# Three token tiles instead of two in step at the start of a linear-attention and gMLP mixer

## The chip, the core and the metric

The kernel runs on one core of a Trainium2 chip. The metric is the time of one execution in microseconds (us), measured on the device. TensorE (PE in the profile) multiplies matrices into PSUM; VectorE (DVE), ScalarE (ACT) and GpSimd (POOL) read PSUM or SBUF and do the element-wise work; SyncE (SP) here only issues DMAs, as ScalarE does for some.

## What is computed

Two mixers run on the same input x of 2048 tokens by 512, and a per-token gate mixes them. The reference, cut to what matters:

```python
def _A_ref(x, wqkv, w_phi, wo):          # B, S, D = 1, 2048, 512; 32 heads of 16
    q, k, v = split(x @ wqkv)
    pq, pk = q @ w_phi, k @ w_phi        # per head
    phi_q = concat([softmax(pq), softmax(-pq)])
    phi_k = concat([softmax(pk), softmax(-pk)])
    kv, z = phi_k.T @ v, phi_k.sum(tokens)
    return ((phi_q @ kv) / (phi_q @ z + 1e-06)) @ wo
def _B_ref(x, w_in, w_sp, b_sp, w_out):  # F = 1376, Fh = 688
    z = gelu(x @ w_in)
    z1 = z[..., :Fh]
    z2 = layernorm(z[..., Fh:])
    g = w_sp @ z2 + b_sp[:, None]        # over the 2048 tokens
    return (z1 * g) @ w_out
g = sigmoid((x * gate_w).sum(-1, keepdims=True))
return g * _A_ref(...) + (1 - g) * _B_ref(...)
```

## The kernel before

The tokens are cut into 16 tiles of 128. A first stage makes z2 and z1 of every tile: x @ w_in in its two halves of 688 columns, through GELU. A second stage runs attention and the product with w_sp over the stored tiles and writes the output. The order of the instructions on TensorE and ScalarE is the order in which the program writes them; on VectorE and the queues a scheduler decides, and it prefers copies marked high priority.

**The contraction.** x @ w_in contracts over 512, in four blocks `dt` of 128. The right half of w_in (688 columns, for z2) lies in SBUF as `w_z2[:, dt, :]`, and "block dt" below is its 128 by 688 piece. One token tile of z2 takes eight matmuls: four blocks by two column halves `j` of 344 (`z_one`, L190). The second half has one column more, 345, for the gate's logit; `gate_T` (L284) puts gate_w into that column by a tiny transpose on TensorE and a copy on VectorE (L287). z1 uses the left half, `w_z1`, in the same way.

**x transposed.** The matmuls need x with its features on the partitions (`xT`). For tokens of tiles 4 to 15 a DMA transpose brings it (L130 one tile each, L139 four tiles). For tiles 0 to 3 a plain load brings x into `xs`; `x_T` (L274) then transposes 128-column pieces on TensorE (L276) into a PSUM tile from the pool's two `pq` buffers, and VectorE (L282) or ScalarE (L279) copies the result into `xT`.

**PSUM for z.** There are three `zp` tiles of two banks, taken in turn. After a tile's eight matmuls, `z2_out` (L203) runs GELU on ScalarE (L205), the copy of the gate logit to `glog` on VectorE (L206), and the batch-norm statistics on VectorE (L208, L209). A zp tile is free for its next user after GELU and the glog copy. z1 tiles use the same three buffers and only GELU (L256).

**The opening.** `z2_first_two` (L214) writes the order by hand: filler matmuls on constants (`warm_up`, L221), the transposes of x tiles 0 and 1, then blocks 0 and 1 of the first column half of both tiles, the gate, block 2, the second column half, and x tile 2's transposes; then tile 0 and tile 1 are finished, and x tile 3 is transposed. The first pair of transposes of x tile 1 writes to an extra PSUM tile `tp1` that borrows the third zp. After it, `z2_tile(2)` and `z2_tile(3)` run alone, and then a loop over chunks of four tiles: z2 (from the second chunk on), z1, and the normalisation (L263 to L268).

**The queues.** Two DMA queues carry the first loads. On Sync's: x tile 0 (L119), x tile 1 (L121), x tiles 2 and 3 in one DMA (L123), the second half of block 0 (L126), the transpose for tile 4 (L130), the two halves of w_z1 (L134), then the further transposes. On ScalarE's: the first half of block 0 (L120) and blocks 1, 2, 3 (L117). These DMAs signal on eight completion semaphores in turn, so the ninth is issued once the first has landed. GpSimd's queue brings gate_w (L113).

**Later.** `load_out_weights` (L423) loads w_out and wo into parts of `wspT` that the second stage has finished with; wo comes as two DMAs (L430).

Of the kernel before, what the change touches and what calls it, by code (L numbers as in the profile page):

```python
# [11 lines left out]
BF16 = mybir.dt.bfloat16  # L12
I32 = mybir.dt.int32

P = 128
# [4 lines left out]
F = 1376  # L20
FH = 688
HF = FH // 2
NT = S // P
NDT = D // P
# [11 lines left out]
def kernel(  # L36
# [14 lines left out]
    nc = tc.nc  # L51
    x2 = A_x.flatten_outer_dims()
# [11 lines left out]
    w_z2 = early.tile([P, NDT, WP], BF16, name="w_z2")  # L64
# [26 lines left out]
    xs = early.tile([P, 4, D], BF16, name="xs")  # L91
# [4 lines left out]
    w_in_v = B_w_in.rearrange("(dt p) f -> p dt f", p=P)  # L96
# [7 lines left out]
        out=ramp[:, 0, :], data0=ones32[:, :], data1=zeros[:, :], initial=0.0,  # L104
# [4 lines left out]
    for q in range(4):  # L109
        qs = slice(32 * q, 32 * q + 32)  # L110
        nc.vector.tensor_tensor(
            out=ident[qs, qs], in0=ramp[qs, 0, :], in1=ramp[qs, 1, :], op=ALU.is_equal)
# [3 lines left out]
    def load_z2w(eng, dt):  # L116
        eng.dma_start(out=w_z2[:, dt, 0:FH], in_=w_in_v[:, dt, FH:F])  # L117

    nc.sync.dma_start(out=xs[:, 0, :], in_=x2[0:P, :])  # L119
    nc.scalar.dma_start(out=w_z2[:, 0, 0:HF], in_=w_in_v[:, 0, FH:FH + HF])  # L120
    nc.sync.dma_start(out=xs[:, 1, :], in_=x2[P:2 * P, :])  # L121
    load_z2w(nc.scalar, 1)
    nc.sync.dma_start(  # L123
        out=xs[:, 2:4, :], in_=x2[2 * P:4 * P, :].rearrange("(i p) d -> p i d", p=P))
    load_z2w(nc.scalar, 2)
    nc.sync.dma_start(out=w_z2[:, 0, HF:FH], in_=w_in_v[:, 0, FH + HF:F])  # L126
    load_z2w(nc.scalar, 3)

    def x_dma_T(i):
        nc.sync.dma_start_transpose(out=xT[:, :, i * P:(i + 1) * P], in_=x2[i * P:(i + 1) * P, :])  # L130

    x_dma_T(4)
    for h in range(2):
        nc.sync.dma_start(  # L134
            out=w_z1[:, 2 * h:2 * h + 2, :], in_=w_in_v[:, 2 * h:2 * h + 2, 0:FH])
    for i in range(5, 8):
        x_dma_T(i)
    for q in range(2, NCH):
        nc.sync.dma_start_transpose(  # L139
            out=xT[:, :, q * CH:(q + 1) * CH], in_=x2[q * CH:(q + 1) * CH, :]  # L140
        )
    nc.sync.dma_start(out=brow[0:NT, :], in_=B_b_sp.rearrange("(t p) -> t p", p=P))
    for qk in (1, 0):
        nc.sync.dma_start_transpose(
            out=wqkT[:, qk * NDT:(qk + 1) * NDT, :], in_=A_wqkv[:, qk * D:(qk + 1) * D])
# [4 lines left out]
    for h in range(2):  # L150
        nc.sync.dma_start(
            out=wv_sb[:, 2 * h:2 * h + 2, :],
            in_=A_wqkv[h * 2 * P:(h + 1) * 2 * P, 2 * D:3 * D].rearrange("(dt p) n -> p dt n", p=P),
        )
    for q in range(NCH):
        nc.sync.dma_start_transpose(
            out=wspT[:, :, q * CH:(q + 1) * CH], in_=B_w_sp[q * CH:(q + 1) * CH, :]
# [4 lines left out]
        out=mask4[:], in_=mask4[:], pattern=[[-32, NG]],  # L162
# [3 lines left out]
        out=mask4[:], in_=mask4[:], pattern=[[32, NG]],  # L166
# [3 lines left out]
        out=mask64[:, :, :], in_=mask4[:, :, None].to_broadcast([P, NG, DH]))  # L170
# [4 lines left out]
    psA = psA_cm.__enter__()  # L175
    turn = {"zp": 0, "pq": 0, "mm": 4}

    def next_turn(kind, n):
        turn[kind] += 1
        return f"{kind}{(turn[kind] - 1) % n}"  # L180

    def zp_tile():
        return psA.tile([P, 2, CH], FP32, name="zp", tag=next_turn("zp", 3))

    def pq_tile(shape, dtype=FP32):
        return psF.tile(shape, dtype, name="pq", tag=next_turn("pq", 2))

    def z_one(zp, tt, wt, w, dt, j, first=0):
        n = HF if j == 0 else w - HF
        nc.tensor.matmul(  # L190
            zp[:, j, 0:n], lhsT=xT[:, dt, tt * P:(tt + 1) * P],
            rhs=wt[:, dt, j * HF:j * HF + n],
            start=(dt == first), stop=(dt == NDT - 1),
        )

    def z_mm(tt, wt, w):
        zp = zp_tile()
        for dt in range(NDT):
            for j in range(2):
                z_one(zp, tt, wt, w, dt, j)  # L200
        return zp

    def z2_out(tt, zp):  # L203
        z2v = z2all[:, tt, :].rearrange("p (j n) -> p j n", j=2)
        nc.scalar.activation(out=z2v, in_=zp[:, :, 0:HF], func=AF.Gelu_apprx_tanh)  # L205
        nc.vector.tensor_copy(out=glog[:, tt:tt + 1], in_=zp[:, 1, HF:HF + 1])  # L206
        for j in range(2):
            nc.vector.bn_stats(out=bn6[:, tt, j, :], in_=z2v[:, j, :])  # L208
        nc.vector.bn_aggr(out=mv[:, tt, :], in_=bn6[:, tt, :, :].rearrange("p j s -> p (j s)"))  # L209

    def z2_tile(tt):
        z2_out(tt, z_mm(tt, w_z2, FH + 1))

    def z2_first_two():  # L214
        zps = [zp_tile() for _ in range(2)]
        tp1 = psA.tile([P, 2, P], BF16, name="tp1", tag=next_turn("zp", 3))
        turn["zp"] -= 1

        def warm_up(n, w=CH):
            for _ in range(n):  # L220
                nc.tensor.matmul(  # L221
                    zps[0][:, 1, 0:w], lhsT=nc.const_aps.tensor(1.0, [P, P], BF16),
                    rhs=nc.const_aps.tensor(1.0, [P, w], BF16), start=True, stop=True)

        def one(tt, dt, j):
            z_one(zps[tt], tt, w_z2, FH + 1, dt, j, first=j)

        warm_up(6)
        warm_up(2, P)
        x_T(0, 0, 1, pq_tile([P, 1, P], BF16)[:, :, :])  # L230
        x_T(0, 1, NDT, pq_tile([P, 3, P], BF16)[:, :, :])
        warm_up(3, P)
        one(0, 0, 0)
        x_T(1, 0, 2, tp1[:, :, :])
        x_T(1, 2, NDT, pq_tile([P, 2, P], BF16)[:, :, :], on_act=True)
        one(0, 1, 0)
        warm_up(1, P)
        one(1, 0, 0)
        one(1, 1, 0)
        gate_T()  # L240
        one(0, 2, 0)
        one(1, 2, 0)
        for dt in range(1, 3):
            one(0, dt, 1)
            one(1, dt, 1)
        x_T(2, 0, NDT, pq_tile([P, NDT, P], BF16)[:, :, :])
        for tt in range(2):
            one(tt, 3, 0)
            one(tt, 0, 1)
            one(tt, 3, 1)  # L250
            z2_out(tt, zps[tt])
        x_T(3, 0, NDT, pq_tile([P, NDT, P], BF16)[:, :, :])

    def z1_tile(tt):
        zp = z_mm(tt, w_z1, FH)
        nc.scalar.activation(  # L256
            out=z1all[:, tt, :].rearrange("p (j n) -> p j n", j=2), in_=zp[:, :, 0:HF],
            func=AF.Gelu_apprx_tanh,
        )
# [14 lines left out]
    def x_T(i, d0, d1, tp, on_act=False):  # L274
        for dt in range(d0, d1):
            nc.tensor.transpose(tp[:, dt - d0, :], xs[:, i, dt * P:(dt + 1) * P], ident[:, :])  # L276
        dst = xT[:, d0:d1, i * P:(i + 1) * P]
        if on_act:
            nc.scalar.copy(out=dst, in_=tp)  # L279
        else:  # L280
            with tc.high_priority():
                nc.vector.tensor_copy(out=dst, in_=tp)  # L282

    def gate_T():  # L284
        gt = pq_tile([P, NDT])
        nc.tensor.matmul(gt[:, :], lhsT=gaterow[:, :], rhs=ident[:, 0:NDT], start=True, stop=True)
        nc.vector.tensor_copy(out=w_z2[:, :, FH], in_=gt[:, :])  # L287

    def b_T():
        bt = pq_tile([P, NT])  # L290
        nc.tensor.matmul(bt[:, :], lhsT=brow[:, :], rhs=ident[:, 0:NT], start=True, stop=True)
        nc.vector.tensor_copy(out=bT[:, :], in_=bt[:, :])
# [20 lines left out]
        return [lambda: take(dst[:, 2], banks[2]), lambda: take(dst[:, 3], banks[3])]  # L313

    with tc.manual_schedule(engines={mybir.EngineType.PE, mybir.EngineType.Activation}):
        z2_first_two()
        z2_tile(2)
        z2_tile(3)
        for c in range(NCH):
            ts = list(range(c * 4, c * 4 + 4))  # L320
            for tt in ts:
                if c > 0:
                    z2_tile(tt)
                if c >= 2 and tt % 4 == 1:
                    later = fold(3 - c)
            for tt in ts:
                z1_tile(tt)
                if c >= 2 and tt % 2 == 0:
                    later.pop(0)()
            z2_norm(ts)  # L330
            if c == 1:
                b_T()
# [90 lines left out]
    def load_out_weights():  # L423
        slabs = wspT[:, :, 0:D]
        w_main = [slabs[:, 0:5, :], slabs[:, 5:10, :]]
        w_rem, wo_t = slabs[:, 10, :], slabs[:, 11:11 + NDT, :]
        nc.gpsimd.memset(w_rem, 0.0)
        for h in range(2):
            gs = slice(2 * h, 2 * h + 2)
            nc.sync.dma_start(  # L430
                out=wo_t[:, gs, :],
                in_=A_wo[h * 2 * P:(h + 1) * 2 * P, :].rearrange("(g p) n -> p g n", p=P))
        for i in range(2):
            nc.sync.dma_start(
                out=w_main[i],
                in_=B_w_out[i * REM:i * REM + 5 * P, :].rearrange("(ft p) n -> p ft n", p=P),
            )
        nc.sync.dma_start(out=w_rem[0:REM, :], in_=B_w_out[5 * P:FH, :])
        nc.sync.dma_start(out=w_rem[P - REM:P, :], in_=B_w_out[0:REM, :])
        return w_main, w_rem, wo_t  # L440
# [95 lines left out]
    with tc.manual_schedule(engines={mybir.EngineType.PE, mybir.EngineType.Activation}):  # L536
# [3 lines left out]
        for tt in range(NT):  # L540
# [7 lines left out]
            if tt == 7:  # L548
                w_main, w_rem, wo_t = load_out_weights()
# [51 lines left out]
```

The softmax here doesn't subtract the row's maximum and nothing guards it: scores larger than these inputs give would overflow.

## Time and profile before

| what | value |
|---|---|
| median of 5 runs | 208.56 us (208.14 to 209.03) |
| the profiled execution's own time | 208.72 us |
| its span, first to last instruction | 207.0 us |
| TensorE busy | 202.7 us, 98% |
| VectorE busy | 129.5 us, 63% |
| ScalarE busy | 76.5 us, 37% |
| GpSimd busy | 45.3 us, 22% |
| z stage's matmuls (L190), 256 of them | 39.3 us busy |

The span leaves out 1.72 us of the profiled execution's time, which lie around its first and last instruction. In the timelines a line gives start, duration, engine, source line, operation, what it writes and reads, shape and count; in square brackets stands how long the engine was idle before it, and what ended that. Matmuls overlap each other: the stated duration of one is its way through the array, and the distance from one start to the next is what it holds the engine for. DMA issues are listed with their size and the median time from issue to landing.

### The profile page before, as it was taken

The page shows a single profiled execution, that of the slowest core. Times are in us where ns is not written, and L with a number is a line of the kernel's source. Part 1 is how long each engine was busy: PE and PEld are TensorE (multiplying, and loading weights), DVE is VectorE, ACT ScalarE, POOL GpSimd, SP SyncE. Part 2 cuts the span into 40 slices and gives each one's busy share as a digit, 9 for nine tenths or more (in the row PEclk, how much of TensorE's full clock was granted, in tenths as well). Part 3 has the DMA queues.
Part 4 walks back from the last instruction along what each step waited for, and adds up shares of the span by engine and source line. Part 5 has one row for each costly group of instructions (what it writes and reads, how often), then busy time and mean ns, then how long its engine had stood idle before and what let it go on. Part 6 is the DMA issues. An engine that isn't in the chain of part 4 may idle for free.

```text
span 207.0 us, 3966 instructions
## 1 busy us (share of the span) xinstructions
PE 202.7 (98%) x1544; PEld 120.9 (58%) x1544; DVE 129.5 (63%) x278; ACT 76.5 (37%) x123; POOL 45.3 (22%) x73
## 2 busy tenths in 40 slices
PE   8999999999999999999999999999999999999994
PEld 4566666655566555556565666555455555665642
DVE  3377756655977778879797788555466553633330
ACT  2666678786422232333323033222251126001322
POOL 5020202020542326243342422222204220200000
PEclk9999999999999999999999999999999999999999
DMA  6999399999995024971413226753564667453642
GB/s 186 271 225 193 85 232 209 254 180 273 179 290 122 3 38 93 331 102 31 89 22 70 50 41 114 145 104 73 106 160 89 79 104 189 54 104 73 128 90 78
DMA packets 89315, 27.22 MB, mean 131 GB/s; under 512 B 83184, under 2 KB 89296, under 8 KB 89296
## 3 DMA queue, kind: packets, MB, share of 16 engines
q1 hardware_dynamic: 86384, 24.28, 61.0%
q10 hardware_dynamic: 2880, 2.68, 4.0%
q8 instruction: 12, 0.20, 0.4%
q14 instruction: 7, 0.06, 0.1%
q0 software_dynamic: 32, 0.00, 0.0%
HBM read 4.41 MB, written 2.10 MB: 31 GB/s over the span
## 4 chain that ended last, share of the span: by engine, by line
PE 95%; DMA 2%; ACT 1%; ACTq 0%; DVE 0%; issue 0%
PE mm L445 36%; PE zp L190 17%; PE mm L350 14%; PE mm L484 8%; PE mm L482 7%; PE mm L390 7%; DMA w_z<-in_B_w_in_dram 2%; PE at L458 2%; PE kvacc L406 2%; PE mm L487 1%; PE zp L303 0%; ACT z1all L256 0%; ACT wq_p L310 0%; ACTq L117 0%; PE pq L276 0%; ACTq L120 0%
## 5 line engine op out<-in xcount | busy, mean ns | idle before, releaser
L445 PE MATMUL mm<-z2all,wspT 128*128 128x344 bf16 x512 | 79.9, 309 | 0.0
L445 PEld LDWEIGHTS <-wspT 128*128 128x128 bf16 x512 | 49.0, 98 | 25.7 <-issue 0.4
L190 PE MATMUL zp<-w_z,xT 128*128 128x344 bf16 (+1 forms) x256 | 39.3, 312 | 0.5 <-DMA w_z<-in_B_w_in_dram 0.5
L354 ACT ACTIVATE eq<-mm 128x512 bf16<-128x512 f32 x32 | 17.4, 594 | 51.3 <-POOL eq L367 21.5
L358 DVE TENSOR_REDUCE zs<-eq 128x64 f32<-128x1024 bf16 x16 | 19.5, 1220 | 20.3 <-ACT eq L354 20.3
L190 PEld LDWEIGHTS <-xT 128*128 128x128 bf16 x256 | 24.9, 99 | 12.5 <-issue 0.6
L450 DVE SCALAR_TENSOR_TENSOR ucat<-mm,bT,z1all 128x344 bf16<-128x344 f32 x32 | 17.4, 544 | 21.9 <-PE mm L445 21.9
L367 POOL TENSOR_TENSOR eq<-eq,ratio 128x512 bf16<-128x512 bf16 x16 | 16.9, 1055 | 50.0 <-DVE ratio L366 41.8
L354 ACT ACTIVATE ek<-mm 128x512 bf16<-128x512 f32 x32 | 17.3, 601 | 27.4 <-PE mm L350 27.4
L498 ACT ACTIVATE ob<-mm,g_inv 128x512 bf16<-128x512 f32 (+1 forms) x16 | 10.9, 680 | 32.8 <-PE mm L487 28.0
L358 DVE TENSOR_REDUCE zs<-ek 128x64 f32<-128x1024 bf16 x16 | 19.3, 1209 | 2.8 <-ACT ek L354 2.8
L484 PE MATMUL mm<-wspT,uT 128*128 128x512 bf16 (+2 forms) x85 | 20.1, 366 | 0.0
L350 PEld LDWEIGHTS <-xT 128*128 128x128 bf16 x128 | 12.2, 98 | 13.2 <-PE mm L487 0.8
L367 POOL TENSOR_TENSOR ek<-ek,ratio 128x512 bf16<-128x512 bf16 x16 | 16.9, 1057 | 2.3 <-DVE ratio L366 1.8
L482 PE MATMUL mm<-wspT,oT 128*128 128x512 bf16 (+2 forms) x68 | 16.6, 366 | 0.0
L350 PE MATMUL mm<-wq_p,xT 128*128 128x512 bf16 x64 | 16.4, 379 | 0.0
L390 PE MATMUL mm<-wv_sb,xT 128*128 128x512 bf16 x64 | 16.4, 379 | 0.0
L350 PE MATMUL mm<-wk_p,xT 128*128 128x512 bf16 x64 | 16.3, 379 | 0.1
L208 DVE BATCH_NORM_STATS2 bn<-z2all 128x6 f32<-128x344 bf16 x32 | 14.9, 501 | 0.0
L205 ACT ACTIVATE z2all<-zp 128x688 bf16<-128x688 f32 x16 | 11.8, 743 | 7.1 <-PE zp L190 7.1
L256 ACT ACTIVATE z1all<-zp 128x688 bf16<-128x688 f32 x16 | 11.9, 744 | 5.1 <-PE zp L190 4.7
L484 PEld LDWEIGHTS <-uT 128*128 128x128 bf16 x85 | 8.2, 98 | 9.2
(72 smaller groups left out, 145.1 us busy)
## 6 DMA issues: line engine op xcount, KB each, us to landing
out_dram<-ob ACTq DMA_DIRECT2D x15, 128.0 KB, 1.7
wspT<-in_B_w_out_dram SPq DMA_DIRECT2D x2, 640.0 KB, 4.8
w_z<-in_B_w_in_dram SPq DMA_DIRECT2D x2, 344.0 KB, 4.3
w_z<-in_B_w_in_dram ACTq DMA_DIRECT2D x3, 172.0 KB, 4.9
wv_sb<-in_A_wqkv_dram SPq DMA_DIRECT2D x2, 256.0 KB, 3.5
wspT<-in_A_wo_dram SPq DMA_DIRECT2D x2, 256.0 KB, 3.9
xs<-in_A_x_dram SPq DMA_DIRECT2D x2, 128.0 KB, 2.7
xs<-in_A_x_dram SPq DMA_DIRECT2D x1, 256.0 KB, 5.1
```

The source lines that it names most:

```text
L190: nc.tensor.matmul(zp[:, j, 0:n], lhsT=xT[:, dt, tt * P:(tt + 1) * P], rhs=wt[:, dt, j * HF:j * HF + n], start=(dt == first), stop=(dt == ...
L208: nc.vector.bn_stats(out=bn6[:, tt, j, :], in_=z2v[:, j, :])
L256: nc.scalar.activation(out=z1all[:, tt, :].rearrange("p (j n) -> p j n", j=2), in_=zp[:, :, 0:HF], func=AF.Gelu_apprx_tanh,)
L350: nc.tensor.matmul(ps[:, :], lhsT=xT[:, dt, tt * P:(tt + 1) * P], rhs=w[:, dt, :], start=(dt == 0), stop=(dt == NDT - 1))
L354: nc.scalar.activation(out=e[:, :, a, :], in_=ps[:, :].rearrange("p (h f) -> p h f", f=DH), func=AF.Exp, scale=1.0 - 2.0 * a)
L358: nc.vector.tensor_reduce(out=z[:].rearrange("p h a -> p (h a)"), in_=e[:].rearrange("p h a f -> p (h a) f"), axis=AX.X, op=ALU.add,)
L367: nc.gpsimd.tensor_tensor(out=e[:, :, 1, :], in0=e[:, :, 1, :], in1=ratio[:, :, None].to_broadcast([P, H, DH]), op=ALU.mult)
L390: nc.tensor.matmul(v_ps[:, :], lhsT=xT[:, dt, tt * P:(tt + 1) * P], rhs=wv_sb[:, dt, :], start=(dt == 0), stop=(dt == NDT - 1))
L445: nc.tensor.matmul(gp[:, 0:HF], lhsT=wspT[:, st, tt * P:(tt + 1) * P], rhs=z2all[:, st, j * HF:(j + 1) * HF], start=(st == 0), stop=(st == ...
L450: nc.vector.scalar_tensor_tensor(out=ucat[tt % NU][:, c0 + j * HF:c0 + (j + 1) * HF], in0=gp[:, 0:HF], scalar=bT[:, tt:tt + 1], in1=z1all[ ...
L482: nc.tensor.matmul(acc, lhsT=oT[:, g, :], rhs=wo_t[:, g, c0:c1], start=(g == 0), stop=False)
L484: nc.tensor.matmul(acc, lhsT=uT[:, i + ft, :], rhs=w_main[i][:, ft, c0:c1], start=False, stop=False)
```

## The change

Three things change at the start, and one later.

- The loads: x tile 2 is a DMA of its own on Sync's queue, third there, and block 2 follows it on that queue. ScalarE's queue carries both halves of block 0, then blocks 1 and 3. x tile 3 comes behind these on Sync's queue, then w_z1. The DMA transpose for tile 4 moves behind w_z1, to those of tiles 5 to 7.
- The opening takes three token tiles instead of two: all three zp tiles are taken at once, x tiles 1 and 2 are transposed in the same way (first pair copied by VectorE, second pair by ScalarE), and each block is used for all three tiles before the next. tp1 and the reordered accumulation (`first`) go. x tile 3 is transposed before the last two matmuls of tile 2.
- Only `z2_tile(3)` is left to run alone after it. On VectorE, by the compiled order, the copy of x tile 3 stands ahead of tile 0's glog copy; before, that glog copy stood ahead of it.
- wo is loaded by one DMA.

```diff
--- before.py
+++ after.py
@@ -119,21 +119,20 @@
     nc.sync.dma_start(out=xs[:, 0, :], in_=x2[0:P, :])
     nc.scalar.dma_start(out=w_z2[:, 0, 0:HF], in_=w_in_v[:, 0, FH:FH + HF])
     nc.sync.dma_start(out=xs[:, 1, :], in_=x2[P:2 * P, :])
+    nc.scalar.dma_start(out=w_z2[:, 0, HF:FH], in_=w_in_v[:, 0, FH + HF:F])
+    nc.sync.dma_start(out=xs[:, 2, :], in_=x2[2 * P:3 * P, :])
     load_z2w(nc.scalar, 1)
-    nc.sync.dma_start(
-        out=xs[:, 2:4, :], in_=x2[2 * P:4 * P, :].rearrange("(i p) d -> p i d", p=P))
-    load_z2w(nc.scalar, 2)
-    nc.sync.dma_start(out=w_z2[:, 0, HF:FH], in_=w_in_v[:, 0, FH + HF:F])
+    load_z2w(nc.sync, 2)
     load_z2w(nc.scalar, 3)
+    nc.sync.dma_start(out=xs[:, 3, :], in_=x2[3 * P:4 * P, :])

     def x_dma_T(i):
         nc.sync.dma_start_transpose(out=xT[:, :, i * P:(i + 1) * P], in_=x2[i * P:(i + 1) * P, :])

-    x_dma_T(4)
     for h in range(2):
         nc.sync.dma_start(
             out=w_z1[:, 2 * h:2 * h + 2, :], in_=w_in_v[:, 2 * h:2 * h + 2, 0:FH])
-    for i in range(5, 8):
+    for i in range(4, 8):
         x_dma_T(i)
     for q in range(2, NCH):
         nc.sync.dma_start_transpose(
@@ -185,12 +184,12 @@
     def pq_tile(shape, dtype=FP32):
         return psF.tile(shape, dtype, name="pq", tag=next_turn("pq", 2))

-    def z_one(zp, tt, wt, w, dt, j, first=0):
+    def z_one(zp, tt, wt, w, dt, j):
         n = HF if j == 0 else w - HF
         nc.tensor.matmul(
             zp[:, j, 0:n], lhsT=xT[:, dt, tt * P:(tt + 1) * P],
             rhs=wt[:, dt, j * HF:j * HF + n],
-            start=(dt == first), stop=(dt == NDT - 1),
+            start=(dt == 0), stop=(dt == NDT - 1),
         )

     def z_mm(tt, wt, w):
@@ -211,10 +210,8 @@
     def z2_tile(tt):
         z2_out(tt, z_mm(tt, w_z2, FH + 1))

-    def z2_first_two():
-        zps = [zp_tile() for _ in range(2)]
-        tp1 = psA.tile([P, 2, P], BF16, name="tp1", tag=next_turn("zp", 3))
-        turn["zp"] -= 1
+    def z2_first_three():
+        zps = [zp_tile() for _ in range(3)]

         def warm_up(n, w=CH):
             for _ in range(n):
@@ -223,7 +220,11 @@
                     rhs=nc.const_aps.tensor(1.0, [P, w], BF16), start=True, stop=True)

         def one(tt, dt, j):
-            z_one(zps[tt], tt, w_z2, FH + 1, dt, j, first=j)
+            z_one(zps[tt], tt, w_z2, FH + 1, dt, j)
+
+        def x_T_split(i):
+            x_T(i, 0, 2, pq_tile([P, 2, P], BF16)[:, :, :])
+            x_T(i, 2, NDT, pq_tile([P, 2, P], BF16)[:, :, :], on_act=True)

         warm_up(6)
         warm_up(2, P)
@@ -231,25 +232,27 @@
         x_T(0, 1, NDT, pq_tile([P, 3, P], BF16)[:, :, :])
         warm_up(3, P)
         one(0, 0, 0)
-        x_T(1, 0, 2, tp1[:, :, :])
-        x_T(1, 2, NDT, pq_tile([P, 2, P], BF16)[:, :, :], on_act=True)
-        one(0, 1, 0)
-        warm_up(1, P)
+        x_T_split(1)
+        warm_up(2, P)
         one(1, 0, 0)
-        one(1, 1, 0)
+        x_T_split(2)
+        warm_up(2, P)
+        one(2, 0, 0)
         gate_T()
-        one(0, 2, 0)
-        one(1, 2, 0)
-        for dt in range(1, 3):
-            one(0, dt, 1)
-            one(1, dt, 1)
-        x_T(2, 0, NDT, pq_tile([P, NDT, P], BF16)[:, :, :])
-        for tt in range(2):
+        for tt in range(3):
+            one(tt, 1, 0)
+        for dt in range(2):
+            for tt in range(3):
+                one(tt, dt, 1)
+        for j in range(2):
+            for tt in range(3):
+                one(tt, 2, j)
+        for tt in range(3):
+            if tt == 2:
+                x_T(3, 0, NDT, pq_tile([P, NDT, P], BF16)[:, :, :])
             one(tt, 3, 0)
-            one(tt, 0, 1)
             one(tt, 3, 1)
             z2_out(tt, zps[tt])
-        x_T(3, 0, NDT, pq_tile([P, NDT, P], BF16)[:, :, :])

     def z1_tile(tt):
         zp = z_mm(tt, w_z1, FH)
@@ -313,8 +316,7 @@
         return [lambda: take(dst[:, 2], banks[2]), lambda: take(dst[:, 3], banks[3])]

     with tc.manual_schedule(engines={mybir.EngineType.PE, mybir.EngineType.Activation}):
-        z2_first_two()
-        z2_tile(2)
+        z2_first_three()
         z2_tile(3)
         for c in range(NCH):
             ts = list(range(c * 4, c * 4 + 4))
@@ -425,11 +427,7 @@
         w_main = [slabs[:, 0:5, :], slabs[:, 5:10, :]]
         w_rem, wo_t = slabs[:, 10, :], slabs[:, 11:11 + NDT, :]
         nc.gpsimd.memset(w_rem, 0.0)
-        for h in range(2):
-            gs = slice(2 * h, 2 * h + 2)
-            nc.sync.dma_start(
-                out=wo_t[:, gs, :],
-                in_=A_wo[h * 2 * P:(h + 1) * 2 * P, :].rearrange("(g p) n -> p g n", p=P))
+        nc.sync.dma_start(out=wo_t, in_=A_wo.rearrange("(g p) n -> p g n", p=P))
         for i in range(2):
             nc.sync.dma_start(
                 out=w_main[i],
```

## The prediction

> **What bounds the kernel now.** I read the page's busy shares and its chain first, then the list of what TensorE waited for, then the timeline of the first 13 us, because that is where the diff works.
>
> ```profile
> PE 202.7 (98%) x1544; PEld 120.9 (58%) x1544; DVE 129.5 (63%) x278; ACT 76.5 (37%) x123; POOL 45.3 (22%) x73
> ...
> PE 95%; DMA 2%; ACT 1%; ACTq 0%; DVE 0%; issue 0%
> ```
> ```profile
> PE zp L221 <- PEq L585: 0.8, 1, 0.8
> PE zp L190 <- DMA w_z<-in_B_w_in_dram: 0.5, 1, 0.5
> ```
> TensorE is the bound: it makes 95% of the chain, and after its start it waits once, 0.49 us for weight block 2. From 6.71 us on it never stops for another engine. So the time is the opening plus a fixed queue of matmuls, and a shift of the queue at its beginning reaches the end one to one. My mark is the first matmul of token tile 3.
>
> The timeline shows why the opening is slow (start, duration, instruction):
> ```profile
> 4.32 0.49 PE L190 MATMUL zp<-w_z,xT 128*128 128x344 bf16 x1
> 4.61 0.42 PE L276 MATMUL tp<-ident,xs 128*128 128x128 bf16 x2
> ...
> 5.06 0.29 DVE L282 COPY xT<-tp 128x256 bf16<-128x256 bf16 x1 [0.46 <-PE tp L276]
> 5.28 0.37 ACT L279 COPY xT<-pq 128x256 bf16<-128x256 bf16 x1 [1.26 <-PE pq L276]
> ...
> 5.42 0.78 PE L190 MATMUL zp<-w_z,xT 128*128 128x344 bf16 x2
> 5.67 1.28 ACT L205 ACT_TABLE_LOAD   x1
> ...
> 6.00 0.21 PE L286 MATMUL pq<-ident,gaterow 128*128 128x4 bf16 x1
> ...
> 6.28 0.17 DVE L287 CAST w_z<-pq 128x4 bf16<-128x4 f32 x1 [0.92 <-PE pq L286]
> 6.71 0.31 PE L190 MATMUL zp<-w_z,xT 128*128 128x344 bf16 x1 [0.49 <-DMA w_z<-in_B_w_in_dram]
> ```
> The 344-column matmul at 4.32 is followed by the transpose at 4.61, so it holds TensorE 0.29 us; after 6.71 a tile of eight takes 1.17 us, 0.146 each. A 128-column transpose falls from 0.107 to 0.056 us in the same way. The array runs at half rate until about 6.65 us in this execution. (The granted-clock column reads 1.00 before that too; the durations decide.)
>
> The handover of the PSUM tiles is the third thing:
> ```profile
> 8.44 1.38 ACT L205 ACTIVATE z2all<-zp 128x688 bf16<-128x688 f32 x2 [1.50 <-PE zp L190]
> ...
> 9.22 0.16 DVE L206 COPY glog<-zp 128x1 f32<-128x1 f32 x1 [0.79 <-ACT z2all L205]
> 9.30 0.41 DVE L282 COPY xT<-pq 128x512 bf16<-128x512 bf16 x1
> 9.74 0.94 DVE L208 BATCH_NORM_STATS2 bn<-z2all 128x6 f32<-128x344 bf16 x2
> 10.28 0.74 ACT L205 ACTIVATE z2all<-zp 128x688 bf16<-128x688 f32 x1 [0.45 <-PE zp L190]
> ```
> There are three zp tiles. Token tile 3 takes the one of tile 0, so it needs tile 0's GELU and its glog copy done. Before, the copy ends at 9.38 and tile 3 starts at 10.08: 0.7 us to spare. (10.28, tile 2's GELU, lies 0.35 after that tile's last matmul, 0.146 long.)
>
> **The change, step by step.** All starts are of this execution.
>
> *Loads.* Tile 4's DMA transpose, which went out at 3.55 amid the weight loads, now goes out behind the two w_z1 loads; x tile 2 is a load of its own, and block 2 moves from ScalarE's queue to Sync's. The DMA issues give what I need: 128 KB of x takes 2.7 us median to land, 86 KB of block 0 2.7, a 172 KB block 4.9 median, the 256 KB pair 5.1. The two x tiles landed at 3.3 and 4.3, so a third behind them should land near 5.2 (an estimate: one more step of 0.94 us); its bounds are 1.74+2.7=4.4 and, if it takes as long as the old pair, 6.86. I take 5.2. Block 1 has 86 KB more ahead of it: 4.4 becomes about 4.9, needed at 6.76. Block 2, at most 5.4 us after its issue at 2.2, is there at 7.6 and needed at 8.1. Block 3 by 7.6, needed at 9.0. x tile 3 goes out at 3.55, when the first block has landed and its semaphore is free; at 5.1 us it lands at 8.7, needed at 9.6. So the 0.49 us wait goes. The w_z1 halves go out earlier than before (4.9 and 5.5), and the DMA transposes of tiles 4 to 7 and the two large ones behind them keep about their places: tile 4 landed at 8.0, may now land near 10, and is needed near 16. No cost; the cover is several microseconds.
>
> *Opening on TensorE.* Up to 4.61 nothing changes. From the first transpose of x tile 1 (4.61) to the first matmul reading it (5.42) is 0.81: transposes, VectorE copy, semaphore. The second block-0 matmul stays at 5.42; before, blocks 0 and 1 of tile 0 and a filler stood in that gap or around it, now fillers only. It ends at 5.71. Now x tile 2 repeats the same chain at half rate: 5.71+0.81=6.52. Its transposes need ScalarE's copy out of the pq buffer, done at 5.65, which just fits. The matmul of tile 2 straddles the clock: 0.13 of its 0.29 us, then 0.08 at full rate, to 6.73. The gate transpose adds 0.03 (b_T's like matmul at 25.26 is followed at 25.29): 6.76. Three block-1 matmuls: 7.20. The next reads the gate column: cast done 0.45 after the gate matmul (6.00 to 6.45), plus 0.05 for the semaphore: 7.23. So the opening has spent its 0.49 us gain on the second copy chain.
>
> *The middle.* Twelve matmuls, 1.76: 8.99. Tile 0's last two: the second starts at 9.13 where it was 8.10. Tile 1's two end at 9.57, four transposes of x tile 3 at 9.80, tile 2's two at 10.09. By the matmul count tile 3 could start at 10.09, against 10.08 before: the change is worth nothing up to here. ScalarE's table load moves from 5.67 to about 6.8 and ends near 8.1, hidden until 9.48; uncovered it would cost up to 1.28.
>
> *The new wait.* Tile 0 now finishes only 0.96 us ahead of tile 3. Its GELU runs 9.13+0.35=9.48 to 10.22. In VectorE's written order x tile 3's copy now stands ahead of the glog copy: it starts 0.26 after the last transpose (9.74), at 10.00, takes 0.42, and glog follows 0.03 later, 10.45 to 10.61; with 0.05 for the semaphore tile 3 starts at 10.66. Wait: 0.57. All later matmuls queue behind it on TensorE. If the order of the two copies did not matter, the GELU alone would still hold tile 3 until about 10.46 (GELU end, 0.03, copy 0.16, 0.05): 0.37. Without any wait the bound is zero. I take 0.57. The next handover, tile 1's zp to the first z1 tile, is ready near 11.6 (two batch-norm steps of 0.43 and a copy behind glog) and needed at 11.83: 0.2 us to spare.
>
> *The rest.* Three more fillers lie in the copy chains, and the accumulation starts at block 0 in both halves, which changes no count. wo comes as one DMA of 512 KB instead of two of 256 (3.9 us each): issued near 81 us, first used at 129; the uT transpose behind it slips by at most those 3.9 us. No cost.
>
> **Sum:** 10.66−10.08=+0.58. The profiled execution took 208.72 (span 207.0 and 1.72 around it), which gives 209.30; on the median of 208.56 it is 209.14. I say 209.2.
>
> [...]
>
> **The rivals.**
> *Clock earlier.* If full rate holds from 4.61, each copy chain takes 0.66 (transpose 0.06, 0.26, copy 0.29, 0.05) instead of 0.81 and each matmul 0.146: 5.27, 5.42, 6.08, 6.23, gate column at 6.7. That is 0.5 earlier, while the kernel before still waits for block 2 until 6.7. Net +0.06: 208.6, not slower. It decides from a rate change at or before 4.6 us; in between it is pro rata. For it: the rate change may differ between runs, which spread over 0.9 us. Against it: the one record has 6.65.
> *x tile 2 late.* If it lands at 6.86 instead of under 5.71, the opening slips 1.15 further: 210.3; every microsecond past 5.71 counts in full. A clock coming later costs half of its delay. For: three loads share the first microseconds with the weights. Against: the 0.94 us step.
> *Faster.* The handover is hidden and the clock early together: −0.57 and −0.52 from 10.66, 9.57, so 208.05; more only if the runs of before wait longer for block 2 than the profiled one, which its time, above the median, does not suggest.
>
> **How the numbers follow.** A measurement here can tell about 0.3% (0.63 us) from no change. Forecast, 208.9 to 209.5: 0.58, of it 0.34 beyond 209.19 and 0.24 below, since later clock and second handover only add. x tile 2 or the clock late, 209.5 to 210.4: 0.16, slower. Clock earlier, 208.5 to 208.9: 0.16, no change. Faster rival, below 208.4: 0.10, of it 0.07 under 207.93. Slower 0.50, same 0.43, faster 0.07. The range 208.4 to 209.9 leaves out the faster rival and less than half of the late one.
>
> **What would show it.** Right: no wait for w_z; a gap of about 0.16 us before tile 2's first matmul; tile 0's GELU at 9.5; tile 3's first matmul held by DVE glog for about 0.57; the first z1 GELU at 13.2 instead of 12.61. Wrong: tile 3 starting without a wait, a wait for xs, or 344-column matmuls at 0.15 us before 5 us.

## The result and the profile after

| | before | after |
|---|---|---|
| median | 208.68 us (207.88 to 211.07, 79 runs) | 209.39 us (208.94 to 211.75, 44 runs) |
| the profiled execution | 208.72 us, span 207.0 | 210.28 us, span 208.6 |
| first matmul of token tile 3 | 10.08 us | 11.67 us |
| first z1 GELU | 12.61 us | 14.20 us |

The ratio is 1.0036, with a 95% interval of 1.0027 to 1.0045: the change costs about 0.7 us, and the interval straddles the 0.3% that the prediction set as its bound. The profiled execution of after lies 0.9 us above the median of its kernel, so its opening must be read as a late one.

The busy shares and the chain, on the page of after:

```profile
PE 203.1 (97%) x1547; PEld 120.9 (58%) x1547; DVE 128.7 (62%) x278; ACT 76.7 (37%) x124; POOL 45.3 (22%) x73
...
PE 94%; DMA 3%; ACT 1%; DVE 1%; SPq 0%; issue 0%
```

TensorE is still the bound, but DMA and VectorE have each taken one percent more of the chain. The list of what TensorE waited for in after (total, times, longest, us) says where:

```profile
PE pq L279 <- DMA xs<-in_A_x_dram: 1.2, 1, 1.2
PE zp L218 <- PEq L583: 0.8, 1, 0.8
PE zp L189 <- DVE glog L205: 0.3, 1, 0.3
PE zp L189 <- DVE xT L285: 0.2, 1, 0.2
```

The wait for `w_z` is gone. In its place stand a wait for an x tile, a wait for `glog`, and the small one for the second copy chain. The DMA issue that the first waits for is the third load on Sync's queue, x tile 2; the answer for its line in after:

```profile
L123 SPq DMA_DIRECT2D xs<-in_A_x_dram x1: 424/424/424, 1.7 to 1.7; - x1
...
DMA to landing us min/median/max: 5.3/5.3/5.3
```

It was issued at 1.74 us and landed at 7.02. In this record 14 of its 16 completion signals came by 5.70 us and the last two at 6.97 and 7.02. The timeline of after shows what this did:

```profile
5.41 0.47 PE L189 MATMUL zp<-w_z,xT 128*128 128x344 bf16 x1
...
7.07 0.40 PE L279 MATMUL pq<-ident,xs 128*128 128x128 bf16 x4 [1.18 <-DMA xs<-in_A_x_dram]
...
7.74 0.32 PE L189 MATMUL zp<-w_z,xT 128*128 128x344 bf16 x1 [0.16 <-DVE xT L285]
...
10.61 2.02 ACT L204 ACTIVATE z2all<-zp 128x688 bf16<-128x688 f32 x3 [1.44 <-PE zp L189]
...
10.92 0.46 PE L189 MATMUL zp<-w_z,xT 128*128 128x344 bf16 x2
11.12 0.42 DVE L285 COPY xT<-pq 128x512 bf16<-128x512 bf16 x1 [2.82 <-PE pq L279]
11.46 0.15 DVE L205 COPY glog<-zp 128x1 f32<-128x1 f32 x1
...
11.67 2.50 PE L189 MATMUL zp<-w_z,xT 128*128 128x344 bf16 x16 [0.29 <-DVE glog L205]
```

TensorE is idle from about 5.9 to 7.07 for x tile 2. Later tile 2's two last matmuls begin at 10.92 and 11.07, so tile 3 could start at 11.22, 0.146 after the second. It starts at 11.67: the handover holds it 0.45 us (the bracket shows 0.29 of that, since it counts from the modelled end of the last matmul). On VectorE the order is as forecast: x tile 3's copy, then `glog`.

So in the profiled pair tile 3 could start 1.14 us later than before (11.22 against 10.08) and then waited 0.45: 1.59, and the executions differ by 210.28−208.72=1.56. A delay of the opening reaches the end one to one. The profiled time less the start of the first z1 GELU is 196.11 us before, 196.08 after, and between 195.91 and 196.26 in the eleven other profiles below that can be read. Everything that follows can therefore be read from the first 13 us.

### The profile page after: what moved, and what is told of

It reads as the page before. It is cut to its first block, busy times and chain, and to the rows that moved or that the text cites. A ratio compares the mean times of both kernels' runs of the same rounds, so it can differ in the third digit from the quotient of the medians.

```text
span 208.6 us, 3973 instructions
## 1 busy us (share of the span) xinstructions
PE 203.1 (97%) x1547; PEld 120.9 (58%) x1547; DVE 128.7 (62%) x278; ACT 76.7 (37%) x124; POOL 45.3 (22%) x73
## 4 chain that ended last, share of the span: by engine, by line
PE 94%; DMA 3%; ACT 1%; DVE 1%; SPq 0%; issue 0%
PE mm L443 36%; PE zp L189 17%; PE mm L352 13%; PE mm L482 8%; PE mm L480 7%; PE mm L392 7%; DMA xs<-in_A_x_dram 3%; PE at L456 2%; PE kvacc L408 2%; PE mm L485 1%; PE zp L306 0%; ACT z1all L259 0%; DVE xT L285 0%; PE pq L279 0%; ACT wq_p L313 0%
## 5 line engine op out<-in xcount | busy, mean ns | idle before, releaser
L352 PEld LDWEIGHTS <-xT 128*128 128x128 bf16 x128 | 12.2, 98 | 13.2 <-PE mm L485 0.8
```

Source lines behind the costliest of these rows:

```text
L352: nc.tensor.matmul(ps[:, :], lhsT=xT[:, dt, tt * P:(tt + 1) * P], rhs=w[:, dt, :], start=(dt == 0), stop=(dt == NDT - 1))
```

## The experiments

Two theories of the loss stand against each other. **Handover:** running three tiles in step makes tile 0 finish so late that its zp tile isn't free when tile 3 wants it. **x tile 2:** a third load on Sync's queue lands too late for where the opening uses it. A third possibility is that the new load order alone hurts, whatever TensorE does. Each ratio is against runs of before on the same chip, with its 95% interval.

### Finish tile by tile

After, but blocks 2 and 3 are used tile by tile, so that tile 0 ends eight matmuls ahead of tile 2 (x tile 3's transposes go behind tile 0):

```diff
-        for j in range(2):
-            for tt in range(3):
-                one(tt, 2, j)
         for tt in range(3):
-            if tt == 2:
+            if tt == 1:
                 x_T(3, 0, NDT, pq_tile([P, NDT, P], BF16)[:, :, :])
-            one(tt, 3, 0)
-            one(tt, 3, 1)
+            for dt in range(2, NDT):
+                one(tt, dt, 0)
+                one(tt, dt, 1)
```

> The changed kernel, but after blocks 0 and 1 each tile takes its blocks 2 and 3 by itself and is handed to GELU at once, and x tile 3 is transposed behind tile 0. Tile 0 then ends four matmuls (0.58 us) earlier, and its GELU and glog copy are done before tile 3 wants its PSUM tile. Handover theory: the wait ahead of tile 3 goes, 0.57 us less than the changed kernel, about 0.15 us or 0.1% over the kernel before. Theory that x tile 2's landing carries the loss: nothing gained beyond what the handover hides behind that landing, the ratio stays near 1.0036. [...]

Measured: 208.76 us, 1.0008 (0.9993 to 1.0022). TensorE's waits in this kernel:

```profile
PE zp L218 <- PEq L581: 0.8, 1, 0.8
PE pq L277 <- DMA xs<-in_A_x_dram: 0.4, 1, 0.4
PE zp L189 <- DVE xT L283: 0.2, 1, 0.2
```

The wait for `glog` is gone, and with it 0.0028 of the ratio, some 0.58 us. The profiles give a smaller share: this execution took 208.84 us, 1.44 less than that of after, and x tile 2 landed 0.98 us earlier (6.04 against 7.02), which leaves 0.46 for the handover. That is still the larger part of the loss. x tile 2 held TensorE 0.36 us here too.

### The change again, for its opening

> The changed kernel once more, for a second profile, since the first profiled execution was 0.9 us over the median. Handover theory: x tile 2 is not waited for, or by less than 0.3 us; the gap ahead of tile 2's first matmul is 0.16 us; tile 3's first matmul waits 0.4 to 0.6 us for DVE. Theory that x tile 2's landing carries the loss: a wait for xs of over 0.5 us again.

Measured: one execution, 209.93 us. x tile 2 landed at 6.66 and TensorE waited 0.9 for it; tile 3 could have started at 10.85 and started at 11.30, again 0.45 later. So the waits of both theories are there; the landing differs from execution to execution, and the handover doesn't.

### The loads alone

Before's order on TensorE with the change's loads (the first hunk of the diff above).

> The kernel before with its order on TensorE, and the loads of the changed kernel alone (x tiles 2 and 3 apart, block 0 whole on ScalarE's queue, block 2 on Sync's, tile 4's DMA transpose behind w_z1). Handover theory: the loss lies in the order on TensorE, so it does not show here; block 1 lands about 0.5 us later than before and block 2 somewhat earlier, so within 0.2 us of the kernel before, ratio 0.999 to 1.001. Theory that the loads carry the loss: 1.002 to 1.004. Theory that x tile 2's landing carries it: like the kernel before, as that order wants x tile 2 only at about 7.6 us.

Measured: 209.28 us, 1.0041 (1.0021 to 1.0060): not what the handover theory expected, but what the theory that the loads carry the loss did. The timeline of the profiled execution, which took 211.03 us, 1.75 above the median:

```profile
5.99 0.31 PE L189 MATMUL zp<-w_z,xT 128*128 128x344 bf16 x1 [1.22 <-DMA w_z<-in_B_w_in_dram]
...
7.39 1.89 PE L189 MATMUL zp<-w_z,xT 128*128 128x344 bf16 x6 [0.74 <-DMA w_z<-in_B_w_in_dram]
```

In this execution before's order wants block 1 near 4.8 us, and with block 0's second half ahead of it on the queue it landed at 5.95. Block 2 held it a second time. The new load order is not free by itself. But its cost here is a wait for weights, which after doesn't have: after first uses block 1 at 7.92 us, when it has landed (7.20). So this isn't where after loses its time.

### Block 1 ahead of block 0's second half

The kernel just shown, with block 1 moved one place forward:

```diff
-    nc.scalar.dma_start(out=w_z2[:, 0, HF:FH], in_=w_in_v[:, 0, FH + HF:F])
-    nc.sync.dma_start(out=xs[:, 2, :], in_=x2[2 * P:3 * P, :])
     load_z2w(nc.scalar, 1)
+    nc.sync.dma_start(out=xs[:, 2, :], in_=x2[2 * P:3 * P, :])
+    nc.scalar.dma_start(out=w_z2[:, 0, HF:FH], in_=w_in_v[:, 0, FH + HF:F])
```

> e2_loads_only with block 1 ahead of block 0's second half on ScalarE's queue, as before; the order on TensorE is that of the kernel before. If e2_loads_only lost its 0.0041 by block 1 landing at 5.95 us where it is wanted at 5.03, the ratio falls back to 0.999 to 1.001 and the first wait for w_z goes. If the loss comes from x tile 2 apart, block 2 on Sync's queue or tile 4's transpose behind, it stays at 1.003 or more.

Measured: 208.85 us, 1.0026 (1.0011 to 1.0042). Its profile has a single wait for `w_z`, of 0.2 us, in an execution of 208.54, 0.3 below the median. The profile went as expected; the ratio didn't fall to 1.000, and its distance from the loads alone lies within the two intervals. What the rest is stays open.

### Tile 4's transpose behind w_z1

Before, with only the DMA transpose moved (in the trace of before its 512 packets of 256 bytes start from 5.5 us on, while packets of the weight blocks start until 6.9, so it might be what makes block 2 late):

```diff
-    x_dma_T(4)
     for h in range(2):
...
-    for i in range(5, 8):
+    for i in range(4, 8):
```

> The kernel before with one part of the change alone: tile 4's DMA transpose issued behind the two w_z1 loads. If its 256-byte packets delay block 2, block 2 lands up to 0.5 us earlier and the 0.49 us wait shrinks: 0.1 to 0.45 us faster than before, ratio 0.998 to 0.9995. If block 2 is late for the bytes ahead of it or a slow queue, no change, 1.000.

Measured: 208.92 us, 1.0015 (0.9991 to 1.0040). TensorE still waited 0.5 us for block 2, which landed at 6.78. Nothing was gained, so the transpose is not shown to be what makes block 2 late; one profile can't rule out a small effect, since the landing varies between executions.

### x tile 2 as the second load of ScalarE's queue

The same edit to the kernel finished tile by tile, and to after:

```diff
-    nc.scalar.dma_start(out=w_z2[:, 0, HF:FH], in_=w_in_v[:, 0, FH + HF:F])
-    nc.sync.dma_start(out=xs[:, 2, :], in_=x2[2 * P:3 * P, :])
+    nc.scalar.dma_start(out=xs[:, 2, :], in_=x2[2 * P:3 * P, :])
+    nc.sync.dma_start(out=w_z2[:, 0, HF:FH], in_=w_in_v[:, 0, FH + HF:F])
```

> The finish tile by tile of e1_finish_by_tile, and x tile 2 as the second load of ScalarE's queue, ahead of block 0's second half, which moves to Sync's queue behind x tile 1. With 214 KB instead of 384 KB up to its end in its queue, x tile 2 should land near 4.2 us instead of 6.0 to 7.0. Theory of two costs (handover 0.57 us, x tile 2's landing about 0.4 us at the full clock): the wait for xs goes, 0.15 to 0.55 us less than e1_finish_by_tile, ratio 0.998 to 1.000. Theory of the handover alone: like e1_finish_by_tile, 1.0008. If block 0's second half or block 1 becomes late in its place: no gain, and a wait for w_z in the list.

> The changed kernel with x tile 2 as the second load of ScalarE's queue and block 0's second half behind x tile 1, nothing else; the handover stays. Theory of two costs: 0.15 to 0.55 us less than the changed kernel, ratio 1.001 to 1.003, and DVE glog still holds tile 3 for about 0.5 us. Handover alone: 1.0036. x tile 2's landing alone: 1.000.

Measured: 208.47 us, 1.0000 (0.9986 to 1.0015), for the first, and 208.93 us, 1.0016 (0.9994 to 1.0038), for after with the edit. Both are what the theory of two costs expected. x tile 2 landed at 4.26 and 4.33 us. TensorE's waits in after with the edit:

```profile
PE zp L218 <- PEq L583: 0.8, 1, 0.8
PE zp L189 <- DVE xT L285: 0.3, 2, 0.2
PE zp L189 <- DVE glog L205: 0.3, 1, 0.3
```

The wait for the x tile is gone and the one for `glog` is left, again 0.45 us, from 9.60 to 10.05. The four kernels make a table of ratios:

| | x tile 2 third on Sync's queue | second on ScalarE's |
|---|---|---|
| blocks 2 and 3 in step | 1.0036 (after) | 1.0016 |
| blocks 2 and 3 tile by tile | 1.0008 | 1.0000 |

Down the columns the handover costs 0.0028 and 0.0016, along the rows the late load 0.0020 and 0.0008. If the runs' intervals are taken as independent, these four differences carry about ±0.0017, ±0.0026, ±0.0024 and ±0.0021, so by times alone only the first is clear of zero; that both costs are there is shown by the waits in the profiles, which come and go with the edits. Both undone, the loss is gone, but there is no gain either.

### wo in one DMA

Before, with the last hunk of the diff alone.

> The kernel before with wo loaded by one DMA, nothing else. All theories: no change, 0.9985 to 1.0015, and no wait of TensorE for wspT.

Measured: 208.79 us, 1.0011 (0.9996 to 1.0027): no difference can be told, and no wait of TensorE for wo or what lies behind it stands in its profile.

### The third tile's copy chain off the path

If both waits are only undone, what is left of the forecast is that the second copy chain eats the 0.49 us gained on block 2. This kernel takes the tile-by-tile finish, sends block 1 ahead of block 0's second half, lets tiles 0 and 1 go through blocks 0 and 1 as before, and transposes x tile 2 behind the gate in one PSUM tile, with four matmuls of tiles 0 and 1 to cover its copy (their second half begins at block 1). Tile 2 then catches up. Its edit on TensorE, from the tile-by-tile kernel:

```diff
         x_T_split(1)
-        warm_up(2, P)
+        one(0, 1, 0)
+        warm_up(1, P)
         one(1, 0, 0)
-        x_T_split(2)
-        warm_up(2, P)
-        one(2, 0, 0)
+        one(1, 1, 0)
         gate_T()
-        for tt in range(3):
-            one(tt, 1, 0)
-        for dt in range(2):
-            for tt in range(3):
+        x_T(2, 0, NDT, pq_tile([P, NDT, P], BF16)[:, :, :])
+        for dt in (1, 0):
+            for tt in range(2):
                 one(tt, dt, 1)
+        for dt, j in ((0, 0), (1, 0), (1, 1), (0, 1)):
+            one(2, dt, j)
```

> A version meant to beat both: the finish tile by tile of e1_finish_by_tile; block 1 second on ScalarE's queue, block 0's second half third; and tiles 0 and 1 go through blocks 0 and 1 of the first column half as in the kernel before, while x tile 2 is transposed behind the gate and tile 2 catches up on blocks 0 and 1 before block 2 is touched. No matmul then wants x tile 2 before about 6.1 us or block 2 before about 7.8. Theory of two costs: no wait for xs or w_z, no handover wait, tile 3 starts near 9.75 instead of 10.08: 0.2 to 0.35 us faster than before, ratio 0.998 to 0.9995. If TensorE's half-rate stretch alone sets the opening, 1.000.

Measured: 207.94 us, 0.9976 (0.9961 to 0.9991): faster than before and than after. Its timeline:

```profile
5.73 0.38 PE L277 MATMUL pq<-ident,xs 128*128 128x128 bf16 x4
...
6.15 0.42 DVE L283 COPY xT<-pq 128x512 bf16<-128x512 bf16 x1
6.17 1.92 PE L189 MATMUL zp<-w_z,xT 128*128 128x345 bf16 x12
```

After its start TensorE never waits for another engine, and tile 3 starts at 9.31 us, 0.44 earlier than expected; in this execution the full rate (last section) was there from about 4.9 us: the 344-column matmul at 4.96 lasts 0.31 us, the one at 4.32 lasted 0.49. x tile 2 landed at 5.30, before its transposes. Its line:

```profile
L123 SPq DMA_DIRECT2D xs<-in_A_x_dram x1: 424/424/424, 1.7 to 1.7; - x1
...
DMA to landing us min/median/max: 3.6/3.6/3.6
```

This is the same load in the same place as in after, third on Sync's queue and issued at 1.74 us, where it took 5.3 us. What differs is ScalarE's queue, where block 1 now goes ahead of block 0's second half. In the three profiles with that order and x tile 2 third on Sync's queue it landed at 5.71 (the block 1 experiment), 5.30 (here) and 5.29 (the in-step version below); in the four with the change's order at 7.02, 6.66, 6.18 and 6.04 (a fifth execution with that order, the one of 751.5 us further down, has 5.7). So the landing seems to go with the order on the other queue too; that it is the cause isn't shown.

Against the kernel with both waits undone (1.0000) the ratio is 0.0024 lower, 0.5 us. That the copy chain is the whole of it isn't shown, since the load order changed with it and the moment of full rate varies.

### Before against itself

> The kernel before against itself, to see what a comparison of this length tells from no change: 0.9985 to 1.0015 in every theory; block 2 waited for by 0.2 to 0.6 us.

Measured: 208.75 us, 1.0002 (0.9986 to 1.0017). Its profiled execution took 208.28 us and has no wait for `w_z`: block 2 landed at 6.06. So the 0.49 us that the change set out to remove is there in some executions of before and not in others.

### The fast version with the change's finish

The version above with blocks 2 and 3 in step, as in after:

```diff
+        for j in range(2):
+            for tt in range(3):
+                one(tt, 2, j)
         for tt in range(3):
-            if tt == 1:
+            if tt == 2:
                 x_T(3, 0, NDT, pq_tile([P, NDT, P], BF16)[:, :, :])
-            for dt in range(2, NDT):
-                one(tt, dt, 0)
-                one(tt, dt, 1)
+            one(tt, 3, 0)
+            one(tt, 3, 1)
```

> e9_third_behind with one edit: blocks 2 and 3 in step over the three tiles as in the changed kernel, x tile 3's transposes ahead of tile 2's last two matmuls. Nothing in the opening waits here, so the handover stands alone. Handover theory: tile 3 waits 0.45 us as in the three profiles that had it (0.57 by the prediction), ratio up from 0.9976 by 0.0022, to 0.999 to 1.0005. If the gain of e1_finish_by_tile came from elsewhere: stays at 0.9976.

Measured: 208.46 us, 0.9993 (0.9976 to 1.0010), 0.0017 above the version without it. Its timeline:

```profile
9.41 0.46 PE L189 MATMUL zp<-w_z,xT 128*128 128x344 bf16 x2
9.61 0.42 DVE L285 COPY xT<-pq 128x512 bf16<-128x512 bf16 x1 [2.54 <-PE pq L279]
9.96 0.15 DVE L205 COPY glog<-zp 128x1 f32<-128x1 f32 x1
10.16 1.04 PE L189 MATMUL zp<-w_z,xT 128*128 128x344 bf16 x6 [0.29 <-DVE glog L205]
```

The handover wait comes back with the same shape in an opening that has no other wait: tile 3 could start near 9.70 (9.41 and twice 0.146) and starts at 10.16, 0.46 later. The three pairs with and without it differ by 0.0028, 0.0016 and 0.0017, in the mean 0.0020 or 0.42 us (about ±0.0013, 0.27 us, by their intervals), in line with the 0.45 of the profiles.

### The fast version with block 0 whole first

The fast version with block 0's second half back ahead of block 1 (the edit of the block 1 experiment, reversed).

> e9_third_behind with one edit: ScalarE's queue as in the change, both halves of block 0 ahead of block 1. The second matmul of tile 0 wants block 1 at about 5.0 us; block 1 landed at 5.9 to 7.2 in the profiles with that queue and at 4.2 to 4.4 with the other. Theory that e2_loads_only lost its time to block 1: a wait for w_z of 0.9 us or more, 0.4 to 1.0 us slower than e9_third_behind, ratio 0.9995 to 1.0025. If block 1's place does not matter: 0.9976.

Measured: 210.23 us (210.02 without the profiled execution), 1.0063 (1.0033 to 1.0094), more than expected. Its profiled execution took 751.5 us, so its waits can't be compared with those of the others. Of its eleven other executions five lie between 208.39 and 209.13 and six between 210.02 and 211.34, and in three of these six the granted clock was 0.991 or 0.992 instead of 0.999 to 1.000. That a long wait for block 1 let the clock fall is argued from the loads-alone kernel (below), not shown here.

## Why the prediction held, and by which steps

The sum of +0.58 us stands against +0.71 measured by the medians (0.75 by the ratio). Its one cost, the handover wait, is right and makes 0.45 us of the loss. The rest comes from the load of x tile 2, which the sum put at nothing, less what an earlier full rate gave back. That the total came so near is in part luck: the single errors are larger than what they add up to.

The prediction's own signs say the same. No wait for `w_z`, the gap of 0.16 us and the hold by DVE's `glog` are there as it wrote. But a wait for `xs`, which it named as a sign of being wrong, is there too, and in the profile it makes tile 0's GELU start at 10.61 instead of 9.5 and the first z1 GELU at 14.20 instead of 13.2.

- **The wait for block 2 goes, and the second copy chain takes its place.** Right. There is no wait for `w_z`, and tile 2's first matmul waits 0.16 us. With both other losses undone the ratio is 1.0000, which is the "worth nothing up to here" of the middle part.
- **x tile 2 lands at 5.2.** Wrong; this is the step that failed. It landed at 7.02, 6.66, 6.04 and 6.18 us in the four profiles with the change's loads. The estimate took the 0.94 us between x tiles 0 and 1 as the step to the third, although a row for the old pair gave 6.86; and it left out the order on ScalarE's queue, with which the landing of the same load seems to go (5.29 to 5.71 with block 1 ahead). What the median execution had can be estimated: the profiled one is 0.89 above the median, and if all of that is the landing, it came near 6.13; the second profile (6.66, 0.54 above the median) gives 6.12. The transposes begin 0.05 later, at 6.18, 0.47 after the forecast's 5.71.
- **Block 1 lands at about 4.9.** Wrong as well, and hidden: it landed at 7.20, 6.48, 6.23 and 5.95 us in the same four profiles. With x tile 2 as late as it was, after asked for block 1 only at 7.92; the forecast's 6.76 would have left little or nothing to spare.
- **Full rate at 6.65.** The trace of before doesn't give that time: its gate matmul at 6.00 is still slow (0.21 us, 0.17 in after) and the next matmul, at 6.71, is fast (0.31 us, where the one at 5.42 takes 0.49), so the change lies between. In after the full rate was there for x tile 2's work, though the forecast ran the copy chain at half rate. From x tile 2's transposes to the point where tile 3 could start the forecast has 10.09−5.71=4.38 us, after 11.22−7.07=4.15: 0.23 less. The copy chain took 0.67 (7.07 to 7.74), as the early-clock rival had it (0.66).
- **The new wait of 0.57.** Right in place and cause, 0.12 too large: 0.45 in after and in two other profiles, 0.46 in a third. The mis-sized term is the step from the x tile 3 copy to `glog`. The forecast lets `glog` start 0.03 after that copy's end; it started 0.08 before it, at 11.46 against 11.12+0.42. The rows of before already had such an overlap: `glog` from 9.22 for 0.16, the next copy at 9.30. The other steps held: the copy began 0.51 us after the GELU's start, forecast 0.52.
- **The table load, the second handover, wo.** Right: the load ran from 7.89 to 9.17 with the first GELU at 10.61, no wait stands at the first z1 tile, and the wo kernel shows no difference.

For the profiled pair the corrections are +1.36 (7.07 against 5.71), −0.23 and −0.12, and 0.58+1.36−0.23−0.12=1.59, while the execution was 1.56 longer. For the median, with the estimated landing, they are +0.47−0.23−0.12=+0.12, which makes +0.70 of the forecast; since that landing was itself worked out from the profiled execution's distance to the median, this is no second check.

Of the rivals, "x tile 2 late" came true, and "clock earlier" in part: the rate was still half at 5.03 us in after (the 128-column fillers there take 0.31 us, those at 7.30 take 0.22), so its condition of 4.6 was not met, but x tile 2's chain ran at full rate. They took part of each other back. The chance of 0.16 for the late load was too low: it landed past 5.71 in all four profiles with the change's loads.

The moment of full rate is the part of the forecast that one trace could not give: in the profiles here it came at 3.7 us in one execution and after 6.3 in another (last section). In after it was there with the first of x tile 2's transposes, which start at 7.07, 7.13, 7.19 and 7.24, where those of x tile 1 start 0.107 us apart. What sets the moment no run here shows.

## What to carry to other kernels

Running several tiles in step makes them all finish together: before doing it, subtract the first tile's last matmul from the moment its buffer is wanted again, and count every reader of that buffer, a copy of one column included. Here it was enough to share the early steps and finish tile by tile. A load's place in a queue is a due time: read the landing of the same place and size, with the same loads on the other queue, in several executions, and put the consumer behind work that covers the latest of them, for a copy chain that nothing covers cost here about as much as the 0.49 us wait it replaced (ratio 1.0000 with the two other losses undone).

## What the hardware showed

- **The moment of full rate varies by more than 2.5 us.** TensorE's instructions up to about 4.3 us are the same in all kernels. A 128-column transpose holds TensorE 0.107 us at half rate and 0.056 at full, a 344-column matmul 0.287 and 0.146. Full rate came at 3.7 us in the loads-alone kernel (four transposes from 3.68 take 0.40 us) and between 6.0 and 6.7 in before; in the fast version with the change's finish the four transposes from 6.07 take 0.54 us, between the 0.63 of half rate and the 0.39 of full, so half rate lasted to about 6.3 there (an estimate from these three durations). In six others (after, the finish tile by tile, both kernels with x tile 2 on ScalarE's queue, wo alone, before against itself) it came at times between. Timeline lines of the first 344-column matmul, at full rate in the loads-alone kernel and at half rate in the version with the third tile off the path:

```profile
4.23 0.32 PE L189 MATMUL zp<-w_z,xT 128*128 128x344 bf16 x1
```
```profile
4.32 0.49 PE L189 MATMUL zp<-w_z,xT 128*128 128x344 bf16 x1
```

- **After two waits of about a microsecond half rate came back.** In the loads-alone kernel, after the waits of 1.22 and 0.74 us, 344-column matmuls follow each other at 0.287 us from about 7.6 to 10.4, where 0.146 is full rate; that execution took 211.03 us at a granted clock of 0.990. A run of after that took 211.75 has 0.992. A single wait of 1.18 us, in the profile of after, was not followed by it. That the waits are the cause is the author's reading of this one profile; no run shows it.
- **In both waits for a load that the traces of before and after hold, TensorE started after the last of 16 signals.** In before the last two of block 2's came at 6.14 and 6.66 us and its matmul started at 6.71. In after two of x tile 2's came 1.3 us behind the other fourteen (6.97 and 7.02 against 5.70), and blocks 1 to 3 of that execution show the same pattern (block 1: 7.16 and 7.20 against 5.92); the transposes began at 7.07, after the last. Such stragglers aren't the whole of the lateness: in the loads-alone kernel the sixteen are spread from 4.92 to 6.18 us with none far behind. Why they lag wasn't tried.
